# Router logits one token tile at a time, expert norms ahead of the loop, squares behind the routing steps

## The chip, the cores and the metric

The kernel runs on one core of one Trainium2 chip. The metric is the device time of one execution in microseconds (us); for the kernel before it is 814.74 us, the median of three runs (814.07 to 815.54).

## What is computed

Random-feature attention over 4 batches, 8 heads, 576 tokens, head size 64 with 128 features, then a mixture of 8 experts with one expert per token, then a gated feed-forward block. Cut to what matters here:

```python
def phi(x):
    proj = np.einsum('bhsd,md->bhsm', x, omega)
    sq = np.sum(x * x, axis=-1, keepdims=True) / 2.0
    h = proj - sq
    return np.exp(h - np.max(h, axis=-1, keepdims=True)) / np.sqrt(m)
kv = np.einsum('bhsm,bhsd->bhmd', phi(k), v);  z = np.sum(phi(k), axis=2)
x = einsum(phi(q), kv) / (einsum(phi(q), z) + 1e-06)      # 2304 tokens x 512
logits = (x / (norm(x) + 1e-6)) @ (emb / (norm(emb) + 1e-6)).T / tau   # 8 experts
expert_idx = argmax(logits);  gate_w = softmax(logits)[expert_idx]
y = gate_w * (relu(x @ w1[e]) @ w2[e])
out = (silu(y @ w_gate) * (y @ w_val)) @ w_out
```

## The kernel before, in words

The program has three phases. The first (attention and routing) fills about the first 150 us, the second (experts) and the third (gated block) are long streams of matmuls. Only the first is touched.

The 2304 tokens are 18 tiles of 128, in two groups of nine. The first phase is one hand-ordered loop of slots s = 0, 1, 2, ...; the order written in it is the order of each engine's queue. A slot takes one unit of work: nine k tiles of the first group (slots 0 to 8), nine q tiles (9 to 17), nine k tiles of the second group (18 to 26), nine q tiles (27 to 35), then a few slots that only finish older units. For unit s:

- `project` (L433): PE multiplies the tile with omega into a pair of PSUM banks ("two", two buffers).
- `squares` (L399, L403): POOL squares the tile two slots early and, from unit 6 on, adds the squares of each head pairwise from 64 down to 16 columns; `norms` (L412) reduces them on DVE into sh. Before the squares, POOL copies one column of a tile that DVE writes (`mark`, L396), and so waits until DVE has come that far: in the kernel before, until the bias of slot s.
- `maxima` (L443, L448, L451): DVE takes the maximum over the features (mx) and makes the bias; `exps` (L460): ACT makes the features ph.
- k units: `kv_sum` one slot later (L474, PE) accumulates kv; the tile in the middle of a group (MID) belongs to two batches and is done in two halves, one after the other.
- q units: `turn` (L507, PE) transposes ph into two banks of the pool "one" (two buffers); `turned` (L512) copies one bank on DVE and one on ACT (qt); `numerators` (L525, PE) two slots after the projection into the pair "third" (one buffer); `divide` (L536, L539, L540, DVE) makes the token rows x; three slots after, `turn_x` (L554, PE) transposes x, ACT rounds it (L557) and DVE takes the rest (`turned_x`, L561), which gives xp, the hi and lo halves in fp32r.

The router is woven into these slots. `router_stationary` makes the normalised expert matrix en_st: ACT squares emb (L178), then 17 small DVE instructions on 8 partitions (three Newton steps of a root, L144 to L182), one step a slot from slot 2 on; its fp32r halves stand in 16 of 128 columns, the rest are zeros (L166). The class `Routing` multiplies three tiles of xp at a time with en_st (`products`, L218, 384 columns, eight matmuls), copies 16 rows out (L225, lt), transposes them (`logits`, L230) and copies them (L233, lg), all in banks of the pool "one". From slot 21 on one step a slot of `rest` runs on DVE: the norm of the tokens (root_eps again, L144 to L159 on 9 columns), the scaled logits, the first maximum, the gates and the counts, the latter up to slot 34. The names qt, x, xp, lt, lg, mx, bias, sh, ny, nt and mark are those of the rows below.

DMAs are all issued by SP: omega, the k and v tiles, then tau and emb.

Of the kernel before, what the change touches and what calls it, by code (L numbers as in the profile page):

```python
# [10 lines left out]
F32 = mybir.dt.float32  # L11
# [16 lines left out]
def attention_moe_ffn_kernel(  # L28
# [110 lines left out]
    def root_eps(sumsq, parts, n, tag):  # L139


        y = rt.tile([128, n], F32, tag="ny" + tag, name="ny")[:parts]
        t = rt.tile([128, n], F32, tag="nt" + tag, name="nt")[:parts]
        nc.vector.tensor_scalar(  # L144
            out=y.bitcast(I32), in0=sumsq.bitcast(I32), scalar1=1, scalar2=None,
            op0=ALU.logical_shift_right,
        )
        nc.vector.tensor_scalar(
            out=y, in0=y, scalar1=0.97 * 2.0 ** 63.5, scalar2=1e-30, op0=ALU.mult, op1=ALU.max
        )  # L150
        for _ in range(3):
            yield
# [11 lines left out]
    def router_load():  # L164
        nc.sync.dma_start(out=rtau, in_=tau.partition_broadcast(128))
        nc.vector.tensor_copy(  # L166
            en_st.rearrange("p c m -> p (c m)"), zero.to_broadcast([128, NC * 128])
        )
        es = rt.tile([E, DM], F32, name="es")
        nc.sync.dma_start(out=es, in_=emb)  # L170
        return es

    def router_stationary(es):

        e2 = rt.tile([E, DM], F32, name="e2")
        ess = rt.tile([128, 1], F32, name="ess")
        nc.vector.reciprocal(rtau, rtau)
        nc.scalar.activation(out=e2, in_=es, func=AF.Square, accum_out=ess[:E])  # L178
# [4 lines left out]
        yield  # L183
        while clock[0] < PT + 4:
            yield
# [9 lines left out]
    class Routing:  # L195


        def __init__(self, g):
            self.g = g
            self.whole = False  # L200
            self.lg2 = self.small("lg2", PT, 2 * E)

# [3 lines left out]
        def scales(self):  # L206
            g = self.g
            rn = self.rn = yield from root_eps(ss[:, g * PT:(g + 1) * PT], 128, PT, "x")
            yield
            nc.vector.reciprocal(rn, rn)  # L210
            nc.vector.tensor_scalar(out=rn, in0=rn, scalar1=rtau, scalar2=None, op0=ALU.mult)

        def products(self, j):
            c0 = (self.g * PT + 3 * j) * 128
            self.p = bank_of(j == 2 and self.g == 0, 1, 384)[:, 0]
            for c in range(NC):
                for a in range(2):
                    nc.tensor.matmul(  # L218
                        self.p, en_st[:, c, :], xp[:, c, a, c0:c0 + 384],
                        start=(c == 0 and a == 0), stop=(c == NC - 1 and a == 1),  # L220
                    )

        def products_out(self):
            self.lt = rt.tile([2 * E, 384], F32, tag="lt", name="lt", bufs=2)
            nc.vector.tensor_copy(self.lt, self.p[0:2 * E])  # L225

        def logits(self, j):
            p = bank_of(j > 0 and self.g == 0, 3, 2 * E)
            for i in range(3):
                nc.tensor.transpose(  # L230
                    p[:, i, :], self.lt[:, i * 128:(i + 1) * 128], ident[:2 * E, :2 * E]
                )
            nc.vector.tensor_copy(self.lg2[:, 3 * j:3 * j + 3], p)  # L233
            self.whole = j == 2

# [3 lines left out]
        def softmax(self):  # L239
            lg2 = self.lg2  # L240
            lg = self.lg = self.small("lg", PT, E)
            nc.vector.tensor_tensor(out=lg, in0=lg2[:, :, 0:E], in1=lg2[:, :, E:2 * E], op=ALU.add)
# [3 lines left out]
            yield  # L246
            first_max(lm, self.oh, lg, PT, "t")
            yield
            nc.vector.tensor_tensor(out=lg, in0=lg, in1=self.bc(lm), op=ALU.subtract)
            nc.scalar.activation(out=lg, in_=lg, func=AF.Exp)  # L250
# [114 lines left out]
    with p1:  # L365
# [25 lines left out]
        def squares(s, after=None):  # L391
# [72 lines left out]

        def kv_part(s, bt, rows, first, last):
            ph, vt = st[s]["ph"], loads["v", units[s][1]]
            if first and bt % 2:
                a = third()
                acc[bt] = [a[:, j, 0:384] for j in range(2)]
            elif first:  # L470
                acc[bt] = [bank(384) for j in range(2)]
            for h in range(H):
                for f in COLS:
                    nc.tensor.matmul(  # L474
                        acc[bt][h // 4][f, h % 4 * 96:h % 4 * 96 + VW],
                        ph[rows, h, f], vt[rows, h * VW:(h + 1) * VW],
                        start=(first and h % 4 == 0), stop=last, skip_group_check=True,
                    )

        def kv_sum(s):  # L480
            g, i = divmod(units[s][1], PT)
            if i <= MID:
                kv_part(s, 2 * g, slice(0, 128 if i < MID else 64), i == 0, i == MID)
            if i >= MID:
                kv_part(s, 2 * g + 1, slice(0 if i > MID else 64, 128), i == MID, i == PT - 1)

# [29 lines left out]
        def numerators(s):  # L516

            a = third()
            st[s]["a"] = a[:, :, 0:384].rearrange("p a (h w) -> p a h w", w=96)
# [30 lines left out]

        def turn_x(s):
            p = st[s]["xt"] = bank_of(units[s][1] == PT - 1, NC, 128)
            for c in range(NC):
# [11 lines left out]
        om_raw = wk.tile([128, 2 * M], F32, tag="omr", name="om_raw", bufs=1)  # L565
        nc.sync.dma_start(out=om_raw, in_=om)
        load(0)
# [5 lines left out]
        load_v(2)  # L573
        emb_t = router_load()

# [11 lines left out]
        with tc.manual_schedule():  # L587
            p = third()
            for _ in range(8):
# [3 lines left out]
                out=om_s, in0=om_raw, scalar1=SCALE, scalar2=None, op0=ALU.mult  # L593
            )
            squares(0)
            squares(1)
            router = router_stationary(emb_t)
            rest = route[0].rest()
            for s in range(N + 3):
                clock[0] = s  # L600
# [12 lines left out]
                if s < LEAN:  # L613
                    sums(s)
                t = tile_of(s - 6, "q")
                if t is not None and t % 3 == 2:
                    route[-1].logits(t % PT // 3)
                base = s - (2 * PT + 2)
                if base >= 1:
                    next(rest, None)  # L620
                if base == PT + 4:
                    route.append(Routing(1))
                if old is not None:
                    turn_x(s - 3)
                t = tile_of(s - 4, "q")
                group = t is not None and t % 3 == 2
                if group:
                    route[-1].products(t % PT // 3)
                if s > 1:
                    next(router, None)  # L630
# [8 lines left out]
                if group:  # L639
                    route[-1].products_out()  # L640
                if s == PT + 4:
                    next(router, None)
                if tile_of(s - 2, "q") is not None:
# [10 lines left out]
        rest = route[1].rest()  # L654
        route[1].products(2)
        route[1].products_out()
        for _ in range(5):
            next(rest)
        route[1].logits(2)

# [319 lines left out]
```

## Time and profile before

| what | value |
|---|---|
| median of three runs | 814.74 us |
| the profiled execution | 813.87 us |
| its span | 812.1 us |
| PE busy | 792.5 us |
| DVE busy | 524.9 us |
| ACT busy | 273.6 us |
| POOL busy | 190.7 us |
| mean granted PE clock | 0.995 |

The profile's times run from the first instruction of the span; the execution itself is 1.8 us longer than the span. A line of a timeline gives start, duration, engine, source line, operation, output and inputs, shape, and in brackets how long the engine stood idle before it and what ended that. PE durations are latencies of a pipelined engine, so what a stream of matmuls costs is read from the start of one line to the start of the next.

### The profile page before, as it was taken

The page shows a single profiled execution, that of the slowest core. Times are in us where ns is not written, and L with a number is a line of the kernel's source. Part 1 is how long each engine was busy: PE and PEld are TensorE (multiplying, and loading weights), DVE is VectorE, ACT ScalarE, POOL GpSimd, SP SyncE. Part 2 cuts the span into 40 slices and gives each one's busy share as a digit, 9 for nine tenths or more (in the row PEclk, how much of TensorE's full clock was granted, in tenths as well). Part 3 has the DMA queues.
Part 4 walks back from the last instruction along what each step waited for, and adds up shares of the span by engine and source line. Part 5 has one row for each costly group of instructions (what it writes and reads, how often), then busy time and mean ns, then how long its engine had stood idle before and what let it go on. Part 6 is the DMA issues. An engine that isn't in the chain of part 4 may idle for free.

```text
span 812.1 us, 14130 instructions
## 1 busy us (share of the span) xinstructions
PE 792.5 (98%) x5788; PEld 698.8 (86%) x5789; DVE 524.9 (65%) x913; ACT 273.6 (34%) x629; POOL 190.7 (23%) x225
## 2 busy tenths in 40 slices
PE   9999989999999998999999999999999999999998
PEld 8778867899999998998888888888888888888886
DVE  5888989682433433689980079629945993797354
ACT  5798577531322315323233332112212221211120
POOL 3755573300000007222231021202111121111020
PEclk9999999999999999999999999999999999999999
DMA  7645742232423232231220011101200220020014
GB/s 272 201 140 155 224 132 81 64 111 83 101 92 94 79 68 96 89 105 54 77 78 1 0 42 63 53 0 53 78 27 0 79 78 1 26 78 27 1 52 182
DMA packets 23538, 65.69 MB, mean 81 GB/s; under 512 B 3088, under 2 KB 5664, under 8 KB 23464
## 3 DMA queue, kind: packets, MB, share of 16 engines
q1 hardware_dynamic: 23464, 64.69, 25.6%
q8 instruction: 48, 0.79, 0.4%
q14 instruction: 26, 0.21, 0.1%
HBM read 59.89 MB, written 4.79 MB: 80 GB/s over the span
## 4 chain that ended last, share of the span: by engine, by line
PE 61%; DVE 0%; issue 0%
PE two L893 24%; PE one L866 18%; PE third L893 12%; PE two L699 3%; PE third L719 2%; PE two L719 2%; PE third L699 1%; DVE y_acc L875 0%
## 5 line engine op out<-in xcount | busy, mean ns | idle before, releaser
L893 PE MATMUL two<-xp,wp 128*128 128x512 f32 (+1 forms) x960 | 209.5, 368 | 0.0
L893 PEld LDWEIGHTS two<-xp,wp 128*128 128x128 f32 x960 | 168.1, 188 | 31.4 <-DVE s L900 0.6
L866 PE MATMUL one<-wo,h 128*128 128x512 f32 x648 | 159.8, 390 | 0.0
L90 POOL TENSOR_TENSOR h<-s,h 128x512 fp32r<-128x512 f32 (+1 forms) x60 | 78.1, 1303 | 337.7 <-ACT h L89 337.7
L866 PEld LDWEIGHTS one<-wo,h 128*128 128x128 f32 x648 | 120.6, 188 | 24.8 <-DVE y_acc L875 0.3
L875 DVE TENSOR_TENSOR y_acc<-y_acc,one 128x512 f32<-128x512 f32 x90 | 61.5, 684 | 77.3 <-PE one L866 77.1
L893 PE MATMUL third<-xp,wp 128*128 128x512 f32 (+1 forms) x480 | 106.5, 368 | 0.0
L893 PEld LDWEIGHTS third<-xp,wp 128*128 128x128 f32 x480 | 84.4, 188 | 15.4
L460 ACT ACTIVATE ph<-two,bias 128x128 f32<-128x128 f32 x288 | 78.3, 385 | 34.4 <-DVE bias L451 21.2
L699 PE MATMUL two<-xp,wp 128*128 128x288 f32 x576 | 81.8, 300 | 3.7 <-DVEq L784 3.7
L699 PEld LDWEIGHTS two<-xp,wp 128*128 128x128 f32 x576 | 79.2, 192 | 3.9 <-ACT xp L89 3.9
L89 ACT CAST h<-s 128x512 fp32r<-128x512 f32 (+1 forms) x60 | 34.7, 579 | 77.6 <-DVE s L900 77.6
L90 POOL TENSOR_TENSOR xp<-y_f,xp 128x576 fp32r<-128x576 f32 x12 | 19.7, 1678 | 150.7 <-ACT xp L89 150.7
L89 ACT CAST wp<-raw 128x1024 fp32r<-128x1024 f32 x32 | 33.6, 1049 | 63.1 <-PE two L719 35.1
L900 DVE TENSOR_TENSOR s<-two,s 128x512 f32<-128x512 f32 (+1 forms) x40 | 25.3, 633 | 44.3 <-ACT s L899 44.2
L719 PE MATMUL third<-h,wp 128*128 128x288 f32 x384 | 52.5, 296 | 0.0
L899 ACT ACTIVATE s<-two 128x512 f32<-128x512 f32 (+1 forms) x40 | 22.2, 554 | 89.0 <-PE two L893 89.0
L719 PE MATMUL two<-h,wp 128*128 128x288 f32 x384 | 51.8, 296 | 0.0
L719 PEld LDWEIGHTS third<-h,wp 128*128 128x128 f32 x384 | 51.6, 189 | 0.0
L719 PEld LDWEIGHTS two<-h,wp 128*128 128x128 f32 x384 | 51.4, 189 | 0.0
L90 DVE TENSOR_TENSOR wp<-raw,wp 128x1024 fp32r<-128x1024 f32 x30 | 39.1, 1302 | 15.6 <-ACT wp L89 15.6
L443 DVE TENSOR_REDUCE mx<-two 128x8 f32<-128x1024 f32 x36 | 43.8, 1216 | 8.1 <-PE two L433 7.9
(155 smaller groups left out, 927.2 us busy)
## 6 DMA issues: line engine op xcount, KB each, us to landing
raw<-in_w_dram SPq DMA_DIRECT2D x68, 512.0 KB, 3.5
q<-in_qx_dram SPq DMA_DIRECT2D x18, 512.0 KB, 3.6
k<-in_kx_dram SPq DMA_DIRECT2D x14, 512.0 KB, 4.6
v<-in_vx_dram SPq DMA_DIRECT2D x18, 276.0 KB, 4.2
out_dram<-y_acc SPq DMA_DIRECT2D x18, 256.0 KB, 2.0
gate<-gts SPq DMA_DIRECT2D x4, 256.0 KB, 5.3
k<-in_kx_dram SPq DMA_DIRECT2D x3, 256.0 KB, 4.1
k<-in_kx_dram SPq DMA_DIRECT2D x2, 128.0 KB, 2.4
```

Of the source, the lines that this page charges most:

```text
L89: nc.scalar.copy(hi, src)
L90: lo_eng.tensor_tensor(out=lo, in0=src, in1=hi.bitcast(F32), op=ALU.subtract)
L443: nc.vector.tensor_reduce(out=mx.rearrange("p (c a) -> p a c", a=2), in_=p.rearrange("p a (h m) -> p a h m", m=M), axis=AX.X, op=ALU.max,)
L460: nc.scalar.activation(out=ph[:, h, :], in_=p[:, h % 2, h // 2 * M:(h // 2 + 1) * M], func=AF.Exp, bias=bias[:, h:h + 1],)
L699: nc.tensor.matmul(ps[:, j], w[:, a, c, f * 128:(f + 1) * 128], xp[:, c, b, c0 + j * HB:c0 + (j + 1) * HB], start=(c == 0 and n == 0), sto ...
L719: nc.tensor.matmul(ps[:, j], w[:, a, f, :], h[:, b, j * HB:(j + 1) * HB], start=(f == 0 and n == 0), stop=(f == len(hs) - 1 and n == 2),)
L866: nc.tensor.matmul(p, h[:, x, i * 128:(i + 1) * 128], w[:, a, :], start=(k == 0), stop=(k == 3 * GF - 1),)
L875: nc.vector.tensor_tensor(out=dst, in0=dst, in1=p, op=ALU.add)
L893: nc.tensor.matmul(ps[:, m], w[:, a, m, c, :], xp[:, c, x, cols], start=(k == 0), stop=(k == 3 * NC - 1),)
L899: nc.scalar.activation(out=s, in_=ps[:, 0], func=AF.Silu)
L900: nc.vector.tensor_tensor(out=s, in0=ps[:, 1], in1=s, op=ALU.mult)
```

## The change

Six edits of the first phase:

1. omega, tau and emb are issued by ACT's queue, ahead of ACT's table load; SP's queue starts with the first k tile. The zero fill of en_st goes, en_st has 16 columns.
2. The root of the expert norms runs before the slots: ACT squares emb, then squares units 0 and 1 (POOL did these two), and DVE's 17 small instructions stand before the first maximum. The transposes of the expert matrix come at slot 11 and not 13.
3. The router takes one tile a slot: eight fp32r matmuls with 16 stationary columns and 128 moving ones (`products`), one copy of 16x128, one transpose, and one reduction of both halves to eight logits, in columns of the pair "third" that the numerators leave free (384 to 511, and 360 to 375 of its second bank). "third" is taken before the tile's transposes and given to the numerators later in the slot. The last tile of a group is transposed into "third" too.
4. `rest` makes two steps a slot up to slot 26, and POOL's `mark` waits for what that step wrote, if there was one, and not for the bias.
5. Units 23 to 28 keep the full 64 squares a head: POOL adds nothing up, DVE reduces 512 columns.
6. In the MID tile the matmuls of the two batches alternate between column halves of the array.

```diff
-    en_st = rt.tile([128, NC, 128], F32R, name="en_st")
+    en_st = rt.tile([128, NC, 2 * E], F32R, name="en_st")
...
-        nc.sync.dma_start(out=rtau, in_=tau.partition_broadcast(128))
-        nc.vector.tensor_copy(
-            en_st.rearrange("p c m -> p (c m)"), zero.to_broadcast([128, NC * 128])
-        )
+        nc.scalar.dma_start(out=rtau, in_=tau.partition_broadcast(128))
         es = rt.tile([E, DM], F32, name="es")
-        nc.sync.dma_start(out=es, in_=emb)
+        nc.scalar.dma_start(out=es, in_=emb)
...
-        while clock[0] < PT + 4:
+        nc.vector.reciprocal(rtau, rtau)
+        while clock[0] < PT + 2:
...
-        def products(self, j):
-            c0 = (self.g * PT + 3 * j) * 128
-            self.p = bank_of(j == 2 and self.g == 0, 1, 384)[:, 0]
+        def products(self, t, a):
+            self.p = a[0:2 * E, 1, 384:]
             for c in range(NC):
-                for a in range(2):
+                for b in range(2):
                     nc.tensor.matmul(
-                        self.p, en_st[:, c, :], xp[:, c, a, c0:c0 + 384],
+                        self.p, en_st[:, c, :], xp[:, c, b, t * 128:(t + 1) * 128],
...
+        def logits(self, a):
+            self.q = a[:, 1, 360:360 + 2 * E]
+            nc.tensor.matmul(
+                self.q, self.lt, ident[:2 * E, :2 * E], is_transpose=True,
+                start=True, stop=True, skip_group_check=True,
+            )
+        def logits_out(self, t):
+            i = t - self.g * PT
+            nc.vector.tensor_reduce(
+                out=self.lg[:, i], in_=self.q.rearrange("p (a e) -> p e a", a=2),
+                axis=AX.X, op=ALU.add,
+            )
...
-            nc.gpsimd.tensor_tensor(out=sq, in0=xn, in1=xn, op=ALU.mult)
+            if s < 2:
+                nc.scalar.activation(out=sq, in_=xn, func=AF.Square)
+            else:
+                nc.gpsimd.tensor_tensor(out=sq, in0=xn, in1=xn, op=ALU.mult)
             w = D
-            while w > (D // 4 if s > 5 else D):
+            while w > (D // 4 if s > 5 and not 2 * PT + 5 <= s < 3 * PT + 2 else D):
...
-                for f in COLS:
+                for f in range(2):
+                    for n, (bt, rows, first, last) in enumerate(parts):
+                        cols = COLS[(f + n) % 2]
...
-            for s in range(N + 3):
+            for _ in range(4):
+                next(router)
+            for s in range(N + 5):
...
+                wrote = None
                 if base >= 1:
-                    next(rest, None)
+                    for _ in range(2 if s < 3 * PT else 1):
+                        wrote = next(rest, None)
...
+                t, u = tile_of(s - 4, "q"), tile_of(s - 5, "q")
+                inner = tile_of(s - 2, "q") is not None
+                if inner or old is not None or t is not None or u is not None:
+                    a = third()
                 if old is not None:
-                    turn_x(s - 3)
+                    turn_x(s - 3, a)
+                if u is not None:
+                    route[u // PT].logits(a)
+                if t is not None:
+                    route[t // PT].products(t, a)
...
-                    squares(s + 2, st[s]["bias"])
+                    squares(s + 2, st[s]["bias"] if wrote is None else wrote)
...
+                if inner:
+                    st[s - 2]["third"] = a
+                    numerators(s - 2)
+                if t is not None:
+                    route[t // PT].products_out()
+                if u is not None:
+                    route[u // PT].logits_out(u)
+                if inner:
                     divide(s - 2)
```

On DVE at the start of the program, the rows before (ess is the sum of the squared expert rows, om_s the scaled omega):

```order
L166 CAST en_st<-zero 128x512
L592 TENSOR_SCALAR om_s<-om_raw 128x256
L443 TENSOR_REDUCE mx<-two 128x2x4
L448 SCALAR_TENSOR_TENSOR mx<-third,mx 128x2x4
L451 SCALAR_TENSOR_TENSOR bias<-third,mx 128x2x4
```

and the rows now, from the third Newton step on (the rows ahead of these are om_s, the first two steps and the root's start, L144 and L148):

```order
L153 RECIPROCAL nt<-ny 8x1
L154 TENSOR_TENSOR nt<-nt,ess 8x1
L155 TENSOR_TENSOR ny<-ny,nt 8x1
L156 TENSOR_SCALAR ny<-ny 8x1
L159 TENSOR_SCALAR ny<-ny 8x1
L177 RECIPROCAL ny<-ny 8x1
L178 TENSOR_SCALAR es<-es,ny 8x512
L449 TENSOR_REDUCE mx<-two 128x2x4
L454 SCALAR_TENSOR_TENSOR mx<-third,mx 128x2x4
L457 SCALAR_TENSOR_TENSOR bias<-third,mx 128x2x4
```

All seventeen instructions of the expert norms have moved ahead of the first maximum; before, they stood between slots 3 and 7.

On DVE in a q slot, with the waits, the rows before in a slot that ends a group of three tiles:

```order
L451 SCALAR_TENSOR_TENSOR bias<-sh,mx 128x2x4 [waits DVE_49]
L561 TENSOR_TENSOR xp<-one,xp 128x4x128 [waits Activation_49]
L225 COPY lt<-one 16x384 [waits PE_49]
L536 TENSOR_SCALAR r<-third 128x8 [waits PE_49]
L539 RECIPROCAL r<-r 128x8 [waits DVE_49]
L540 TENSOR_TENSOR x<-third,r 128x512 [waits DVE_49]
```

and now in every q slot from slot 14 on:

```order
L457 SCALAR_TENSOR_TENSOR bias<-sh,mx 128x2x4 [waits DVE_49]
L578 TENSOR_TENSOR xp<-one,xp 128x4x128 [waits Activation_49]
L223 COPY lt<-third 16x128 [waits PE_49]
L235 TENSOR_REDUCE lg<-third 128x8
L548 TENSOR_SCALAR r<-third 128x8
L551 RECIPROCAL r<-r 128x8 [waits DVE_49]
L552 TENSOR_TENSOR x<-third,r 128x512 [waits DVE_49]
```

The wait for the numerators has moved from r to lt: r, which reads the numerators, waits for nothing of its own any more, so the copy lt stands until PE has written them.

On POOL in slots 21 and 22, the rows before:

```order
L396 COPY mark<-bias 128x1
L399 TENSOR_TENSOR sq<-k_1389 128x512
L403 TENSOR_TENSOR sq<-sq 128x8x32
L403 TENSOR_TENSOR sq<-sq 128x8x16
L396 COPY mark<-bias 128x1
L399 TENSOR_TENSOR sq<-k_1476 128x512
L403 TENSOR_TENSOR sq<-sq 128x8x32
L403 TENSOR_TENSOR sq<-sq 128x8x16
```

and now, in slots 21 to 24:

```order
L399 COPY mark<-ny 128x1
L405 TENSOR_TENSOR sq<-k_1431 128x512
L399 COPY mark<-ny 128x1
L405 TENSOR_TENSOR sq<-k_1530 128x512
L399 COPY mark<-oh 128x1
L405 TENSOR_TENSOR sq<-k_1602 128x512
L399 COPY mark<-bias 128x1
L405 TENSOR_TENSOR sq<-k_1672 128x512
```

The squares now wait for ny or oh, which DVE's routing step of that slot writes before the maximum, and the two additions are gone there.

## Rows read from the trace of the kernel before

**Rows 1.** Windows of the first phase and after: us, busy time by engine, granted clock, DMA.

```profile
37.46:81.41 43.95, 41.19 (x611) 34.49 (x611) 38.23 (x90) 37.65 (x122) 24.85 (x43) 1.00 0.48 150
81.41:112.90 31.49, 29.63 (x471) 24.85 (x471) 28.85 (x71) 20.00 (x74) 20.27 (x35) 0.95 0.64 195
112.90:141.48 28.58, 25.42 (x361) 20.90 (x358) 25.78 (x73) 23.47 (x76) 12.93 (x22) 1.00 0.29 95
150.00:200.00 50.00, 50.00 (x400) 49.53 (x399) 28.86 (x72) 17.55 (x26) 4.65 (x3) 1.00 0.34 102
```

**Rows 2.** Start: timelines of DVE, ACT and SP; then DMA issues (KB each, us to landing).

```profile
6.02 1.23 DVE L443 TENSOR_REDUCE mx<-two 128x8 f32<-128x1024 f32 x1 [2.80 <-PE two L433]
...
11.85 0.61 ACT L178 ACTIVATE e<-es 8x512 f32<-8x512 f32 x1
...
1.22 1.37 SPq L380 DMA_DIRECT2D k<-in_kx_dram  x3
...
om_raw<-in_om_dram SPq DMA_DIRECT2D x1, 128.0 KB, 2.1
...
rtau<-in_tau_dram SPq DMA_DIRECT2D x1, 0.5 KB, 5.8
```

**Rows 3.** Timeline of DVE, maxima of slots 9 and 11.

```profile
34.41 1.23 DVE L443 TENSOR_REDUCE mx<-two 128x8 f32<-128x1024 f32 x1 [0.55 <-PE two L433]
...
40.06 1.23 DVE L443 TENSOR_REDUCE mx<-two 128x8 f32<-128x1024 f32 x1
```

**Rows 4.** Timeline of DVE, a q slot without router work.

```profile
68.97 0.68 DVE L561 TENSOR_TENSOR xp<-one,xp 128x512 fp32r<-128x512 f32 x1
69.58 0.15 DVE L536 TENSOR_SCALAR r<-third 128x8 f32<-128x8 f32 x1
...
70.61 0.68 DVE L512 COPY qt<-one 128x512 f32<-128x512 f32 x1
71.21 0.28 DVE L412 TENSOR_REDUCE sh<-sq 128x8 f32<-128x128 f32 x1
...
73.06 0.68 DVE L561 TENSOR_TENSOR xp<-one,xp 128x512 fp32r<-128x512 f32 x1
```

**Rows 5.** Router on DVE, 37.46 to 81.41: a copy; waits (total, times, longest).

```profile
59.71 0.54 DVE L225 COPY lt<-one 16x384 f32<-16x384 f32 x1
...
DVE r L536 <- PE third L525: 1.5, 3, 0.7
...
DVE lg L233 <- PE third L230: 1.1, 1, 1.1
```

**Rows 6.** Timeline of PE, a q slot that ends a group of three tiles.

```profile
57.44 0.66 PE L554 MATMUL one<-ident,x 128*128 128x128 f32 x4
57.85 1.67 PE L218 MATMUL one<-xp,en_st 128*128 128x384 f32 x8
59.45 1.15 PE L525 MATMUL third<-kv,qt 128*64 128x65 f32 x32
60.53 1.09 PE L507 MATMUL one<-ident,ph 128*128 128x128 f32 x8
61.55 1.16 PE L433 MATMUL two<-om_s,q 64*128 64x128 f32 x16
```

**Rows 7.** Timeline of PE, fp32r matmuls of 256 columns in the third phase.

```profile
780.51 3.04 PE L893 MATMUL third<-xp,wp 128*128 128x256 f32 x24
```

**Rows 8.** DVE busy by tile and window: ny, cand; nt in two windows.

```profile
81.41:112.90 31.49, 5.99 (x15) 0.95 0.64 195
...
81.41:112.90 31.49, 1.93 (x4) 0.95 0.64 195
...
81.41:112.90 31.49, 3.11 (x9) 0.95 0.64 195
...
157.00:180.00 23.00, 1.61 (x9) 1.00 0.44 129
```

**Rows 9.** Timeline of POOL, squares of a tile in the second k stretch.

```profile
102.22 1.10 POOL L399 TENSOR_TENSOR sq<-q 128x512 f32<-128x512 f32 x1
```

More of the change, by code (lines that the diff above doesn't have):

```diff
@@ L200, in __init__ @@
             self.whole = False
-            self.lg2 = self.small("lg2", PT, 2 * E)
+            self.lg = self.small("lg", PT, E)
         def small(self, name, *shape):
@@ L208, in scales @@
             rn = self.rn = yield from root_eps(ss[:, g * PT:(g + 1) * PT], 128, PT, "x")
-            yield
+            yield rn
             nc.vector.reciprocal(rn, rn)
             nc.vector.tensor_scalar(out=rn, in0=rn, scalar1=rtau, scalar2=None, op0=ALU.mult)
-        def products(self, j):
-            c0 = (self.g * PT + 3 * j) * 128
-            self.p = bank_of(j == 2 and self.g == 0, 1, 384)[:, 0]
+        def products(self, t, a):
+            self.p = a[0:2 * E, 1, 384:]
             for c in range(NC):
-                for a in range(2):
+                for b in range(2):
                     nc.tensor.matmul(
-                        self.p, en_st[:, c, :], xp[:, c, a, c0:c0 + 384],
-                        start=(c == 0 and a == 0), stop=(c == NC - 1 and a == 1),
+                        self.p, en_st[:, c, :], xp[:, c, b, t * 128:(t + 1) * 128],
+                        start=(c == 0 and b == 0), stop=(c == NC - 1 and b == 1),
+                        skip_group_check=True,
                     )
         def products_out(self):
[L224 to L234, printed above, removed]
+            self.lt = rt.tile([2 * E, 128], F32, tag="lt", name="lt", bufs=2)
+            nc.vector.tensor_copy(self.lt, self.p)
+        def logits(self, a):
[10 more added lines that the diff above has]
+            )
+            self.whole = i == PT - 1
         def bc(self, t):
@@ L463, in exps, with kv_parts @@
                 )
-        def kv_part(s, bt, rows, first, last):
+        def kv_parts(s, parts):
             ph, vt = st[s]["ph"], loads["v", units[s][1]]
[L467 to L471, printed above, removed]
-            for h in range(H):
-                for f in COLS:
[L474 to L478, printed above, removed]
+            for bt, _, first, _ in parts:
+                if first and bt % 2:
+                    a = third()
+                    acc[bt] = [a[:, j, 0:384] for j in range(2)]
+                elif first:
+                    acc[bt] = [bank(384) for j in range(2)]
+            for h in range(H):
+                for f in range(2):
+                    for n, (bt, rows, first, last) in enumerate(parts):
+                        cols = COLS[(f + n) % 2]
+                        nc.tensor.matmul(
+                            acc[bt][h // 4][cols, h % 4 * 96:h % 4 * 96 + VW],
+                            ph[rows, h, cols], vt[rows, h * VW:(h + 1) * VW],
+                            start=(first and h % 4 == 0), stop=last, skip_group_check=True,
+                        )
         def kv_sum(s):
             g, i = divmod(units[s][1], PT)
+            parts = []
             if i <= MID:
-                kv_part(s, 2 * g, slice(0, 128 if i < MID else 64), i == 0, i == MID)
+                parts.append((2 * g, slice(0, 128 if i < MID else 64), i == 0, i == MID))
             if i >= MID:
-                kv_part(s, 2 * g + 1, slice(0 if i > MID else 64, 128), i == MID, i == PT - 1)
+                parts.append((2 * g + 1, slice(0 if i > MID else 64, 128), i == MID, i == PT - 1))
+            kv_parts(s, parts)
         def kv_out(s):
@@ L516, in numerators @@
         def numerators(s):
-            a = third()
+            a = st[s]["third"]
             st[s]["a"] = a[:, :, 0:384].rearrange("p a (h w) -> p a h w", w=96)
@@ L549, in token_norms, with turn_x @@
             nc.scalar.activation(out=x2, in_=st[s]["x"], func=AF.Square, accum_out=ss[:, t:t + 1])
-        def turn_x(s):
-            p = st[s]["xt"] = bank_of(units[s][1] == PT - 1, NC, 128)
+        def turn_x(s, a):
+            if units[s][1] == PT - 1:
+                p = a[:, 0].rearrange("p (c t) -> p c t", c=NC)
+            else:
+                p = bank(NC, 128)
+            st[s]["xt"] = p
             for c in range(NC):
@@ L594, in attention_moe_ffn_kernel @@
             )
+            router = router_stationary(emb_t)
+            next(router)
             squares(0)
             squares(1)
-            router = router_stationary(emb_t)
+            for _ in range(4):
+                next(router)
             rest = route[0].rest()
-            for s in range(N + 3):
+            for s in range(N + 5):
                 clock[0] = s
```

37 lines of the change are left out of this document (9 added, 28 removed).

## The prediction

> **What bounds the kernel now.** I read the windows by stage first. From 150 us on PE is busy all the time [rows 1], so nothing that happens in the first phase can be hidden or regained later: the change is worth what it moves the end of that phase, us for us. The borders of the other windows are the starts of the maxima of slots 10, 20, 29 and 35, so a window is a number of slot intervals: ten, nine and six. In all three DVE is the busiest engine by share of work that it cannot overlap with itself (38.2 of 43.95, 28.9 of 31.5, 25.8 of 28.6); PE's 41.2 of 43.95 is a sum of pipelined latencies and reads too high.
>
> Then the timelines. A q slot without router work runs from one xp to the next on DVE in 73.06 - 68.97 = 4.09 us without a gap [rows 4]: DVE sets the pace there. PE needs, in a q slot that holds a group's products, 61.55 - 57.44 = 4.11 from turn_x to the next projection, and some 1.1 for the projection itself (its row has 1.16); the products are 59.45 - 57.85 = 1.60 of it [rows 6]. So PE without router work needs 3.6 a slot and has half a us to spare. A k slot is bound by a ring of PE, DVE and ACT: from the maximum of slot 9 to that of slot 11 it took 40.06 - 34.41 = 5.65, 2.8 a slot, and DVE waited for PE [rows 3]. Wherever k slots take longer than 2.8, DVE has other work in them: the router's small instructions. Those are far dearer than their size. The nine that touch nt took 3.11 us in the second k stretch, beside POOL's squares, and 1.61 for the second group, where POOL does none [rows 8], so 0.18 each when free.
>
> **The sum, stage by stage.** All prices are from the one profiled execution, 813.87 us, which is 0.87 under the median of 814.74; differences are put on the median.
>
> *Start.* The first maximum stands at 6.02 [rows 2]. Now DVE does the 17 instructions of the expert norms ahead of it: 16 at 0.18 [rows 8] and one over 512 columns, priced like lt's 0.54 for 384 [rows 5], make 3.4. They wait for ACT's square of emb, 0.61 [rows 2] and the read of its sum, together some 0.8, and that for emb's landing. emb is third on ACT's queue; three issues on SP took 1.37 [rows 2], so it is issued near 1.7. Landing takes between omega's 2.1 and tau's 5.8 [rows 2]; tau goes just ahead of emb on the same queue, but the queues are nearly empty then, so I take 2.8, near omega's. Maximum at 1.7 + 2.8 + 0.8 + 3.4 = 8.7 (8.0 to 11.7): **+2.7** (+2.0 to +5.7). Squares 0 and 1 on ACT and the missing zero fill lie beside that wait and cost nothing; if emb came at once, project(0) would be the cover.
>
> *First k slots.* From the maximum of slot 0 to that of slot 10 are 37.46 - 6.02 = 31.44. Without the norms between them the slots fall to the ring: five pairs at 5.65, 28.2 in all: **-3.2**. Start and these together are -0.5, between -1.2 and +2.5. The alternating MID matmuls are in the 5.65.
>
> *First q slots (ten intervals, 43.95).* Away go, for the two groups in this window, two copies lt, of 0.54 each with 0.07 overlapped, two copies lg at 0.13, 1.2 in all, and of the waits that DVE has [rows 5] the 1.1 for lg and 0.8 of the 1.5 for r (the other 0.7 is the first numerators' and stays): 3.1. New are, in some 6.5 slots, a copy of 16x128 and a reduction to 8 columns. The trace has neither; between sh's 0.28 for 128 columns [rows 4] and the smallest instructions' 0.18 [rows 8] they are 0.21 and 0.13, 0.34 a slot, 2.2. That makes DVE 4.09 + 0.34 = 4.43 a slot.
>
> Whether PE keeps up with that rests on one price: eight fp32r matmuls of 128 columns. The nearest rows: 24 of 256 columns take 3.04, 0.12 each [rows 7], and a column at the granted clock of 1.00 (2.4 GHz) is 0.42 ns, so 107 of those 120 ns are columns. Taking 256 columns off each of the eight of 384 leaves 1.60 - 0.85 = **0.75**, switches from and to fp32 included. From above: an fp32 transpose of 128 columns takes 1.02 / 8 = 0.128 [rows 6], and a full fp32 product is two passes (the projection's eight matmuls leave 16 records), so eight at full fp32 price would be 2.05. I take 0.75: nothing in 256 or 384 columns departs from one column a cycle. PE then needs 3.6 + 0.75 + 0.1 for one transpose = 4.45. The wait that the change adds: lt stands on DVE until the numerators are written, and r, x, and the next qt are queued behind lt. That makes a ring: qt 0.60 (70.61 to 71.21), turn_x 0.41, transpose 0.1, products 0.75, numerators 1.08 (59.45 to 60.53), lt and lg 0.34, r to x 1.03 (69.58 to 70.61) [rows 4, 6], with 0.2 for three handovers: 4.5. So the slots run at 4.5, 0.08 over DVE's own, 0.5 in six. Window: -3.1 + 2.2 + 0.5 = **-0.4**.
>
> On that added wait: "PSUM — Partial Sum Buffer" of the Trainium skill (section Terms) says that TensorE writing and VectorE reading one bank in one quadrant at the same time is an error. No run here shows it; the order of the instructions agrees, since lt waits for the numerators of its own bank. By a rule that let lt go first, the sum would be 0.7 lower.
>
> *Second k slots (nine intervals, 31.49).* The router's steps there suffered from the squares: the 15 instructions with ny took 5.99 where 15 at 0.2 are 3.0, those with nt 1.5 too much, the four with cand 1.0 [rows 8]: 5.5. With `mark` behind the step, POOL's squares of 1.10 us [rows 9] start under the maximum of 1.23 [rows 3], and I let all 5.5 go. In come sixteen small instructions that stood in slots 29 to 34, at 0.2: +3.2; and in six slots sh from 512 columns, about 0.68 by a line through the maximum's 1.23 for 1024 columns and sh's 0.28 for 128 [rows 3, 4]: +2.4. Per-tile and group work of the router are even here. **+0.1**, between -2 and +3.
>
> *Second q slots (six intervals, 28.58).* The sixteen instructions go, -3.2, and one group's lt, lg and wait for lg, -1.1; per-tile work comes in 4.5 slots, +1.5, the ring in three, +0.3: **-2.5**.
>
> *Behind.* The tail's products and transposes fall under the experts' matmuls as before: 0. SP's queue loses three issues, which are not what its loads wait for: 0.
>
> Sum -0.5 - 0.4 + 0.1 - 2.5 = -3.3: 810.6 against 813.87 in the profile, **811** against the median. Its own range, with the bounds of start and k slots that are not rivals, is 807 to 814.
>
> **Rivals.**
> *Narrow fp32r matmuls are slow (slower).* If 128 columns cost what fp32 costs, products take 2.05 and not 0.75. PE then needs 5.75 a slot and becomes the bound, and DVE's lt stands behind it; of 18 tiles two fall into k slots with room, so 16 x 1.3 = 21 us: 832. For it: no row shows fp32r under 256 columns or with 16 stationary ones. Against: 256, 384 lie on one line. It decides from where products exceed about 0.8 a slot; at half of the way, 1.4, the time would be 821.
> *emb comes late (no change).* With tau's 5.8 us to land the first maximum is at 11.7, and 3 of the 3.3 are lost: 814. For it: tau's tiny pieces stand right ahead of emb on the queue. Against: tau's 5.8 were measured behind eight larger loads. "Trainium Kernel Development and Optimization" of the Trainium skill (section Key Constraints) says that DMAs of all queues run on the same 16 engines and interleave, so that a second issuing engine saves issue time alone; the rows of the start, where SP's issues are 0.45 apart, cannot contradict it, and by it emb shares with the first k tiles, which is this rival.
> *The squares still collide (slower).* If DVE's two-input instructions behind the maximum meet the squares instead, the 5.5 stay: 817. Against: 1.10 us of squares fit under 1.23.
>
> **Numbers.** A measurement of this kernel tells 0.2% (1.6 us) from no change. Forecast 811: 0.54. emb late, 814: 0.12. Narrow matmuls, 821 to 832: 0.27. Collision, 817: 0.07. So faster 0.54, same 0.12, slower 0.34. Cases of both signs hold most of the chance, so the range has to run from the forecast's low end, 807 (the lower bounds of start and k slots together), to the narrow matmuls' 832.
>
> **What would show it.** Right: the eight products of a tile take 0.75 on PE, q slots run at 4.5, DVE waits before lt by a tenth or two, the first maximum is at 8.7, and no routing instruction in the second k slots is over 0.3. Wrong: products near 2 us with DVE waiting over a us before lt; a first maximum past 11; bias or mx instructions of 0.6 and more beside the squares.

## The result and the profile after

| | before | after |
|---|---|---|
| median of four runs | 814.48 us (814.07 to 815.54) | 824.88 us (822.43 to 826.22) |
| ratio to before, 95% interval | | 1.0118 [1.0102, 1.0135] |
| span of the profiled execution | 812.1 us | 821.8 us |
| mean granted PE clock | 0.995 | 0.986 |
| PE busy | 792.5 us | 798.9 us |
| DVE busy | 524.9 us | 524.9 us |

The change made the kernel 1.2% slower; 811 was forecast. The span grew by 9.7 us, where -3.3 was forecast. Cut at the maxima of slots 0, 10, 20, 29 and 35, as the forecast was:

| stage | before | after | difference | forecast |
|---|---|---|---|---|
| start to first maximum | 6.02 | 8.85 | +2.8 | +2.7 |
| first k slots (0 to 10) | 31.44 | 32.51 | +1.1 | -3.2 |
| first q slots (10 to 20) | 43.95 | 46.13 | +2.2 | -0.4 |
| second k slots (20 to 29) | 31.49 | 33.09 | +1.6 | +0.1 |
| second q slots (29 to 35) | 28.58 | 28.50 | -0.1 | -2.5 |
| behind the last maximum | 670.6 | 672.7 | +2.1 | 0 |

These are the windows of the changed kernel (length; busy time and instructions of PE, PE's weight loads, DVE, ACT, POOL; granted clock; DMA share; GB/s); the last three answer to [rows 1]:

```profile
8.85:41.36 32.51, 30.68 (x513) 27.61 (x514) 19.29 (x41) 20.63 (x77) 17.40 (x30) 0.84 0.66 209
...
41.36:87.49 46.13, 43.91 (x651) 36.76 (x652) 39.14 (x99) 37.89 (x123) 25.14 (x43) 0.96 0.44 142
87.49:120.58 33.09, 27.99 (x466) 22.59 (x466) 30.35 (x87) 19.62 (x74) 12.48 (x22) 1.00 0.62 188
120.58:149.08 28.50, 27.05 (x392) 22.94 (x393) 24.25 (x62) 24.16 (x78) 13.53 (x23) 0.94 0.29 94
```

The column to read first is the third from the right, the granted clock. Before, of [rows 1] only the second k window was under 1.00 (0.95). Now the other three stages are. In 2 us windows the first of these stretches looks so:

```profile
8.00:10.00 2.00, 0.15 (x4) 0.00 (x0) 1.90 (x5) 0.00 (x0) 0.00 (x0) 1.00 1.01 380
10.00:12.00 2.00, 1.32 (x16) 1.35 (x16) 1.52 (x4) 1.37 (x6) 1.18 (x2) 0.76 0.92 332
12.00:14.00 2.00, 2.00 (x35) 1.97 (x34) 0.33 (x2) 2.00 (x9) 1.18 (x2) 0.50 0.11 39
...
20.00:22.00 2.00, 2.00 (x30) 2.00 (x28) 0.43 (x1) 0.47 (x2) 0.00 (x0) 0.68 0.52 140
```

PE does next to nothing from 8 to 10 us, then the clock is at half (1.2 GHz) for some 10 us. The timeline of DVE and PE there:

```profile
7.01 1.14 PE L439 MATMUL two<-om_s,k 64*128 64x128 f32 x16
...
8.45 0.47 DVE L178 TENSOR_SCALAR es<-es,ny 8x512 f32<-8x512 f32 x1
8.85 1.21 DVE L449 TENSOR_REDUCE mx<-two 128x8 f32<-128x1024 f32 x1
...
10.68 1.56 PE L428 MATMUL third<-ones,sq 64*128 64x1 f32 x16 [2.53 <-DVE bias L457]
...
14.11 2.08 PE L439 MATMUL two<-om_s,k 64*128 64x128 f32 x16
...
16.24 1.22 DVE L449 TENSOR_REDUCE mx<-two 128x8 f32<-128x1024 f32 x1 [3.58 <-PE two L439]
```

The norms end at 8.9, near the forecast, but PE, with the projection of slot 1 done, waits 2.53 us for the first bias. The next projection then takes 2.08 instead of 1.14, and DVE waits 3.58 for it.

A second stretch begins in slot 11, behind another wait of PE:

```profile
44.12 0.41 PE L185 MATMUL one<-ident,es 8*128 8x8 f32 x4
...
46.74 0.65 PE L519 MATMUL one<-ident,ph 128*128 128x128 f32 x4
...
48.50 0.18 DVE L188 TENSOR_TENSOR en_st<-one,en_st 128x32 fp32r<-128x32 f32 x1
...
48.64 1.12 PE L519 MATMUL one<-ident,ph 128*128 128x128 f32 x4 [1.24 <-DVE qt L524]
49.68 2.08 PE L439 MATMUL two<-om_s,q 64*128 64x128 f32 x16
```

The expert matrix is turned into one of the two banks of the pool "one" in slot 11 (L185) and frees it only with its lo half on DVE in slot 12 (L188). The second half of the turn of ph needs that bank and waits for it: the bracket names the copy qt, which DVE began at 47.90, but L188, right behind it, is what reads the bank. Slot 11, from its maximum to the next, took 7.58 us; before, 4.75.

What the forecast staked most on went well. A slot of the per-tile router:

```profile
65.36 0.65 PE L215 MATMUL third<-xp,en_st 128*16 128x128 f32 x8
...
67.15 0.28 DVE L223 COPY lt<-third 16x128 f32<-16x128 f32 x1 [0.23 <-PE third L537]
67.35 0.15 DVE L235 TENSOR_REDUCE lg<-third 128x8 f32<-128x16 f32 x1
...
69.26 1.22 DVE L449 TENSOR_REDUCE mx<-two 128x8 f32<-128x1024 f32 x1
```

Eight products take 0.65 us (0.59 to the start of the numerators), lt waits 0.23, and the next maximum follows 4.57 us after that of 64.69. In the second k slots five of DVE's small instructions are still long (oc, gt, cand and ext_i are tiles of the routing steps):

```profile
90.51 0.70 DVE L144 TENSOR_SCALAR ny<-ss 128x9 int32<-128x9 int32 x1
...
105.16 1.04 POOL L405 TENSOR_TENSOR sq<-k 128x512 f32<-128x512 f32 x1
...
105.37 0.85 DVE L266 TENSOR_TENSOR oc<-oc,oh 64x8 f32<-64x8 f32 x1
...
109.17 0.77 DVE L275 TENSOR_TENSOR gt<-oh,se 128x72 f32<-128x72 f32 x1
...
112.54 1.04 DVE L127 SCALAR_TENSOR_TENSOR cand<-cand,iota_b 128x16 f32<-128x16 f32 x1
...
116.71 0.89 DVE L309 CAST ext_i<-cnt 1x16 int32<-1x16 f32 x1
```

And behind the loop PE waits once more, in the experts' first matmuls:

```profile
170.54 3.54 PE L720 MATMUL two<-xp,wp 128*128 128x288 f32 x25
174.01 0.23 PE L228 MATMUL third<-ident,lt 16*128 16x16 f32 x1
...
174.54 3.42 PE L720 MATMUL third<-xp,wp 128*128 128x288 f32 x24
...
179.59 0.63 PE L720 MATMUL third<-xp,wp 128*128 128x288 f32 x3 [1.37 <-DVE cand L127]
```

The pair "third" belongs to the router until its last logits at 174; the experts' first "third" pair starts at 174.5 (before: 158.7), and the next one waits 1.37 us for DVE. From the last maximum to the first matmul of the second expert product (189.25) it is 40.17 us; before, 38.17.

### The profile page after: what moved, and what is told of

Read it like the earlier page. It is cut to its first block, busy times and chain, and to the rows that moved or that the text cites. A ratio compares the mean times of both kernels' runs of the same rounds, so it can differ in the third digit from the quotient of the medians.

```text
span 821.8 us, 14331 instructions
## 1 busy us (share of the span) xinstructions
PE 798.9 (97%) x5884; PEld 704.3 (86%) x5885; DVE 524.9 (64%) x934; ACT 275.0 (33%) x631; POOL 180.2 (22%) x211
## 4 chain that ended last, share of the span: by engine, by line
PE 60%; DVE 0%; issue 0%
PE two L914 24%; PE one L887 18%; PE third L914 12%; PE two L720 3%; PE third L740 2%; PE two L740 2%; PE third L720 1%; DVE y_acc L896 0%
```

## The experiments

All start from the changed kernel, but for one. Kernels sent together share the runs of the kernel before, whose median was 815.0 to 815.3 there. The number in brackets is the median of a kernel's executions; every profile is of one execution.

**PE kept busy at the start** (820.05).

```diff
                     project(s)
+                if s == 1:
+                    spare = bank(128)
+                    for _ in range(6):
+                        nc.tensor.matmul(spare, ones, ones, start=True, stop=True)
```

> The changed kernel with six full fp32 matmuls of 128x128 into a free bank behind the projection of slot 1, where PE stood idle for 2.5 us until the first bias; their product is used by nobody. Theory clock (PE's idleness behind the early norms sent the granted clock to half for 10.2 us, which is what slots 1 and 2 cost): no half-clock stretch from 11 us on, slots 1 and 2 fall from 5.79 and 5.33 us to about 3.7 and 3.0, time 824.9 - 4.4 = 820.5. Theory waits (the late first maximum itself, and the ring behind it, cost the time; the clock is a by-product): slots 1 and 2 stay above 5, time 825.

Windows of this run, over the start and from the maximum of slot 0 to that of slot 10:

```profile
8.00:10.00 2.00, 2.00 (x24) 1.88 (x22) 1.85 (x5) 0.00 (x0) 0.00 (x0) 1.00 0.96 314
10.00:12.00 2.00, 2.00 (x42) 1.81 (x41) 1.52 (x4) 1.85 (x8) 1.46 (x4) 1.00 0.81 281
12.00:14.00 2.00, 2.00 (x36) 1.81 (x36) 0.15 (x1) 2.00 (x10) 0.90 (x1) 1.00 0.72 233
...
8.37:36.61 28.24, 28.24 (x531) 24.81 (x528) 19.28 (x41) 20.60 (x77) 17.41 (x30) 1.00 0.80 251
```

Work that nobody uses made the kernel some 4.8 us faster than the change by the medians, 3 by the ratios to the kernel before (1.0080 for 1.0118), 5.0 by the spans of the profiles. Slots 1 and 2 took 3.88 and 2.96, and the ten intervals 28.24 us, the 28.2 of the forecast; in the changed kernel they took 32.51. So the wait cost little by itself, and what it did to the clock cost 4.3.

**The expert matrix in slot 7** (820.31).

```diff
-        while clock[0] < PT + 2:
+        while clock[0] < PT - 2:
...
-                if s >= PT:
+                if s >= PT - 2:
                     next(router, None)
```

> The changed kernel with the transposes of the expert matrix in slot 7 and not 11, and their lo half in slot 8. Theory bank (en_st holds one of the two banks 'one' from slot 11 until DVE comes to the lo half in slot 12, and PE's turn of slot 11 waits 1.2 us for it, after which the clock drops): slot 11 falls from 7.58 to about 4.75, no half-clock stretch at 48.6, time 824.9 - 2.8 = 822. Rival (slot 11 is long because the first numerators wait for ACT's qt behind the exponentials, whatever en_st does): slot 11 stays near 7, half clock stays, 825.

Slot 11 took 4.73, with no half clock there; the ten intervals of the first q slots 43.34, against 46.13 and, before, 43.95: -0.6 where -0.4 was forecast. The bank was the cause. The median fell by 4.6, more than the 2.8 of this slot; the profiled span fell by 3.2.

**The norms back in the slots** (818.33).

```diff
-            for _ in range(4):
-                next(router)
...
-                if s >= PT:
+                if s > 1:
                     next(router, None)
```

> The changed kernel with the expert norms' 17 DVE instructions back in slots 2 to 7, one step a slot; all else as changed. Theory clock: first maximum near 6.0, no half clock before 40 us, maximum of slot 10 at 37.5 as before and not 41.4: 824.9 - 3.9 = 821. If the early norms as I forecast them save what they cost (ring of 2.8 a slot), slots 3 to 8 lengthen by 3 us again and the time is 825 or more.

The stretch from 11 us on is gone; a shorter one came at 26 to 29 us, which the expectation had excluded. The maximum of slot 10 stood at 37.76. Faster than expected, since slot 11 had its wait but no half clock:

```profile
45.05 0.66 PE L519 MATMUL one<-ident,ph 128*128 128x128 f32 x4 [1.25 <-DVE qt L524]
45.63 1.16 PE L439 MATMUL two<-om_s,q 64*128 64x128 f32 x16
```

It took 6.19: of slot 11's 2.8 us in the changed kernel half is the wait (6.19 - 4.73 = 1.5), half the clock (7.58 - 6.19 = 1.4).

**PE kept busy in slot 29** (822.23).

```diff
             for h in range(H):
+                if s == 3 * PT and h == 4:
+                    for _ in range(3):
+                        nc.tensor.matmul(
+                            a[:, 0, 384:], ones, ones, start=True, stop=True, skip_group_check=True
+                        )
```

> The changed kernel with three full fp32 matmuls of 128x128 into spare columns between the two halves of the first numerators of the second group (slot 29), where PE waits 1.37 us for ACT's qt. Theory clock: no half-clock stretch at 123.7, slot 29 falls from 6.40 to about 4.6, time 824.9 - 1.9 = 823. Theory waits: slot 29 stays near 6.4 or grows by the matmuls' 1.2, time 825 to 826.

Slot 29 took 4.94 at full clock, against 6.40 at half. But it took 4.93 and 4.94 in three other kernels without the fill too, whose half-clock stretches lay elsewhere. So the stretch costs 1.5 in this slot; that the fill took it away is not shown.

**Marks behind the routing steps** (821.59). In slots 24 to 27 POOL's mark waits for what the step wrote last:

```diff
-                yield
+                yield oc[:, j - 1] if j else oh[:, 0]
...
-            yield
+            yield cnt[:, 0]
...
-            yield
+            yield dom[:, 0]
```

> The changed kernel, POOL's order alone different: in slots 24 to 27 mark waits for what the routing step of the slot wrote last (oh, oc, cnt, dom) and not for the bias. Theory locks (the four instructions L266 0.85, L275 0.77, L127 1.04 and L309 0.89 us are slow because the squares of the slot before still run beside them; 0.2 each when free): three of the four fall to 0.2 to 0.25 and slots 24 to 27 shorten by 0.6 to 0.8 each, about 2 in all: 824.9 - 2.0 = 823, the maximum of slot 29 2 us earlier against that of slot 20. Rival (they are slow for a reason of their own, such as a 64-partition or a narrow operand): durations and time unchanged. A second rival: squares that come earlier collide with other small instructions instead: less than 1 us.

On DVE's timeline the last four instructions of above are now (the first, L144, stays at 0.70), and ahead of them one has become long:

```profile
102.89 0.69 DVE L454 SCALAR_TENSOR_TENSOR mx<-sh,mx 128x8 f32<-128x8 f32 x1
...
106.68 0.16 DVE L266 TENSOR_TENSOR oc<-oc,oh 64x8 f32<-64x8 f32 x1
...
111.04 0.23 DVE L275 TENSOR_TENSOR gt<-oh,se 128x72 f32<-128x72 f32 x1
...
114.34 0.17 DVE L127 SCALAR_TENSOR_TENSOR cand<-cand,iota_b 128x16 f32<-128x16 f32 x1
...
118.05 0.16 DVE L309 CAST ext_i<-cnt 1x16 int32<-1x16 f32 x1
```

All four fell, so their length was the squares beside them. "SBUF — State Buffer" of the Trainium skill (section Who interferes with whom) says that VectorE, with two inputs in SBUF or in the modes that use two ports, and GpSimd share one pair of ports, which one of them holds for a whole instruction; these rows agree. But the squares that start earlier meet the instruction behind the maximum of slot 23: L454 took 0.17 in the changed kernel, and the slot grew from 2.68 to 3.20. The nine intervals gained only 0.3, 32.79 for 33.09, and this execution had a half-clock stretch at 106 to 110; with the same order and none (all remedies, below) they took 31.75. So the marks are worth 1.3 at full clock, not 2.

**The router's tail in "one"** (818.24).

```diff
-                    a = third()
+                    a = third() if s < N + 2 else bank(1, 512)
```

> The changed kernel with the last three routing slots of the second group (behind the last numerators) in a bank of the pool 'one' and not in 'third'. Theory shared pair (the experts' first 'third' pair cannot start until the router's last logits are out, 174.5 us here and 158.7 before, so two 'third' pairs stand back to back and PE waits 1.4 us for the first to be emptied): first mm2 38.2 to 38.7 us behind the last maximum and not 40.2, time 824.9 - 1.7 = 823. Rival (the tail's extra 2 us are PE's own work for 16-column products and transposes): still 40, time 825.

The experts' first two "third" pairs on PE are apart again, and nothing waits:

```profile
162.94 2.96 PE L720 MATMUL third<-xp,wp 128*128 128x288 f32 x21
...
173.67 3.36 PE L720 MATMUL third<-xp,wp 128*128 128x288 f32 x24
```

The tail fell from 40.17 to 38.50, so 1.7 of its 2.0 was the shared pair. The time fell by more. In the profiled execution the half-clock stretch at the start was shorter than in that of the changed kernel (slots 1 and 2: 5.04 and 2.96) and slot 29 had none (4.93), and no edit explains that.

**POOL's additions back in units 23 to 28** (820.07).

```diff
-            while w > (D // 4 if s > 5 and not 2 * PT + 5 <= s < 3 * PT + 2 else D):
+            while w > (D // 4 if s > 5 else D):
```

> The changed kernel with POOL's two additions back in units 23 to 28, so that DVE reduces 128 columns and not 512 there. By the forecast's prices DVE saves 0.40 in each of six slots (sh 0.27 for 0.67) and POOL's additions, 1.25 us a slot more, meet the small instructions of the next slot. Theory locks: the collisions cost as much as sh saves or more, time 825 to 827. Rival (full-width sh was the dearer choice): 823.

The second k slots took 34.26 for 33.09, a half-clock stretch at 99 to 106 among them. Two slots ahead of it were 0.5 and 0.4 longer for another reason: the squares with their additions outlast the maximum and meet the instruction behind it, 0.17 us elsewhere:

```profile
89.24 1.21 DVE L449 TENSOR_REDUCE mx<-two 128x8 f32<-128x1024 f32 x1
90.48 0.72 DVE L454 SCALAR_TENSOR_TENSOR mx<-sh,mx 128x8 f32<-128x8 f32 x1
```

The four slots behind the stretch were 0.8 shorter together, with DVE reducing 128 columns for 512. So outside the stretch the two orders come out nearly even, and which width is cheaper is not shown: the two slots in the stretch, 1.0 longer, make the difference. The whole time, 820, came out below both theories for other reasons: the half-clock stretch at the start was shorter than in the changed kernel, and slots 11 and 29 had none (6.21 and 4.94).

**The late maximum alone, on the kernel before** (818.01, ratio 1.0052 [1.0034, 1.007]).

```diff
+            scr = wk.tile([128, 1], F32, name="scr", bufs=1)
+            nc.vector.memset(scr, 1.0)
+            for _ in range(31):
+                nc.vector.tensor_scalar(
+                    out=scr, in0=scr, scalar1=1.0, scalar2=None, op0=ALU.mult
+                )
             router = router_stationary(emb_t)
```

> The kernel BEFORE the change with nothing of the change, only 31 small DVE instructions on a scratch tile ahead of the first maximum, so that it stands near 8.8 us and not at 6.0, as in the changed kernel. Theory clock: PE then stands idle for some 2.5 us behind the projection of slot 1, the granted clock falls to half for about 10 us from 10 or 11 us on, and slots 1 and 2 take some 10 us together where they took 6.7: 814.7 + 2.8 + 3 = 820 to 821. Theory waits (a late first maximum costs its own 2.8 us, and DVE's cover behind it gives part of that back): no half clock, 816 to 817.5.

```profile
8.00:10.00 2.00, 0.00 (x0) 0.00 (x0) 1.83 (x7) 0.00 (x0) 0.00 (x0) 1.00 0.58 192
10.00:12.00 2.00, 1.16 (x20) 1.18 (x22) 1.74 (x5) 1.21 (x5) 1.18 (x2) 0.95 0.99 397
12.00:14.00 2.00, 2.00 (x34) 1.88 (x36) 0.34 (x3) 2.00 (x9) 1.18 (x2) 0.50 0.58 234
14.00:16.00 2.00, 2.00 (x28) 2.00 (x30) 0.35 (x1) 1.50 (x6) 0.00 (x0) 0.70 0.51 128
```

With nothing of the change in it, the clock goes to half behind a PE that is idle for 3.0 us, for some 3.4 us in this execution and not 10. Slot 1 took 5.04 for 3.72, the maximum of slot 10 came 4.1 later, 3.0 of it by the later first maximum. The time lies between the two theories; the executions ran from 817.92 to 821.08.

**The router by token tile without the other reorderings** (816.87, 1.0019 [1.0008, 1.0030]). Norms back, expert matrix in slot 8, one routing step a slot, mark behind the bias, additions in all units.

> The changed kernel with the other edits of DVE's and POOL's order undone: norms in slots 2 to 7, squares of units 0 and 1 on POOL, one routing step a slot, mark behind the bias, additions in all units; expert matrix in slot 8. What is left is the router by token tile, the alternating MID matmuls and the issues on ACT. By the forecast's terms (0.75 us of products, slots of 4.5): the loop ends 0.5 to 1.5 us earlier than before, and the tail, which still holds 'third' to the end, gives 2 back: 815 to 816. If the per-tile router itself were the loss: 820 or more.

The last maximum stood at 141.53, before at 141.48: the first q slots -0.6, the second k slots +0.5, the second q slots +0.1. The per-tile router is worth nothing in the loop as a whole in this execution, which had a half-clock stretch at 26 to 29 us, in the first k slots; its tail, 40.19, costs the 2 us. A little slower than expected.

**All remedies** (813.11, 0.9985 [0.9968, 1.0002]): start and slot 29 filled, expert matrix in slot 7, marks, tail.

> The changed kernel with all remedies at once: fill at the start, expert matrix in slot 7, fill in slot 29, marks behind the routing steps, tail in 'one'. If the causes add: 824.9 - 4.4 - 2.8 - 1.9 - 2.0 - 1.7 = 812, under the kernel before (814.5). The half-clock stretches move with every shift of the start, so where one of them falls on PE's path elsewhere, 1.5 to 2 more: 814. If the remedies cover the same time twice: 817.

Its windows behind slot 10, with the granted clock at 1.00; the profile shows no other value in the first phase:

```profile
36.99:80.31 43.32, 41.87 (x647) 35.20 (x648) 38.99 (x98) 37.60 (x122) 25.05 (x43) 1.00 0.48 151
80.31:112.06 31.75, 28.16 (x470) 22.82 (x472) 28.60 (x88) 19.76 (x75) 12.55 (x22) 1.00 0.65 196
112.06:138.90 26.84, 26.24 (x398) 22.24 (x399) 24.33 (x60) 23.81 (x77) 13.33 (x23) 1.00 0.32 100
```

The profiled execution took 811.69 us, 2.2 under that of the kernel before, where -3.3 was forecast; others took up to 817.67. By stages it differs from the kernel before by -0.5 (start and first k slots), -0.6, +0.3, -1.7 and +0.4; the forecast had -0.5, -0.4, +0.1, -2.5 and 0. So at full clock, and with these remedies, the forecast's sum comes out within about 1 us in that execution. As a median the kernel cannot be told from the kernel before.

**The same, and slot 11 filled** (814.06, 0.9999 [0.9980, 1.0018]).

> All remedies as in the run with all at once, and three matmuls more between the halves of the first numerators of the first group (slot 11, where PE still stood idle for 1.3 us). Theory clock: the executions with a half-clock stretch near 45 us become fewer; median 812.5, 0.3% under the kernel before. Rival (slot 11 has nothing to do with those executions): 813.1 as without them.

No gain: twelve executions ran from 810.20 to 818.64, with granted clocks of 0.998 to 0.989.

**All remedies, slot 11 filled, but without the early norms** and without the fill at the start, expert matrix in slot 8 (813.61, 0.9987 [0.9976, 0.9997]).

> All remedies but the early norms: the 17 instructions in slots 2 to 7, no fill at the start. By the forecast the early norms save 0.5 us once PE is kept busy; the run with norms back alone has its maximum of slot 10 at 37.8 and the one with the fill at 36.6, so 1.1: 813 + 1.1 = 814. If the fill's matmuls only move the half-clock stretch elsewhere, no difference: 813.

Ten executions ran from 812.21 to 814.82. The maximum of slot 10 stood at 36.85, between those of the two runs before this one (36.99 and 36.56); as a median it is no slower. So with PE kept busy the early norms gain nothing that shows over norms in the slots. This is the one kernel here whose interval lies under the kernel before, by 0.13%, less than the 0.2% that the forecast took for the least difference to tell.

## Why the prediction was wrong

**Start (+2.7): right, and its end too.** The first maximum stood at 8.85 for 8.7.

**First k slots, "the slots fall to the ring: five pairs at 5.65, 28.2 in all: -3.2": the step that failed.** It is right at full clock (28.24 with PE kept busy) and took PE's pace from rows at a clock of 1.00. That DVE's 3.4 us would leave PE idle for 2.5, and what an idle PE does to the clock, had no term and no rival, though [rows 1] had a window at 0.95. It cost 4.3 of the 13 us between forecast and result, the largest single part. "TensorE: Matmul & The Clock Gate" of the Trainium skill (section What's actually happening) says that half speed is the clock's default state and activity releases it; the run on the kernel before agrees in that the clock fell behind an idle PE and rose with PE busy, and the page would have given a rival here. Nor is the net of -0.5 for start and k slots the norms' doing: with them in the slots the maximum of slot 10 came at 36.85, as early as with them moved and PE kept busy, and before at 37.46. That 0.6 must be due to other edits; the alternating MID matmuls and the issues on ACT's queue were never run alone.

**First q slots (-0.4): products right, one edit not costed.** Products 0.65 for 0.75, slots 4.57 for 4.5, lt's wait 0.23, window -0.6 once the expert matrix is moved. That the transposes of the expert matrix move to slot 11 stands in the change and in no term: 2.8 us, half of it a wait for a bank held over two slots, half the clock.

**Second k slots (+0.1): "I let all 5.5 go" held for what it named, not for what comes in.** The instructions on ny and nt fell from 9.10 us [rows 8] to 5.00 (six stand in both sums), 4.1 of their 4.5; one, at 0.70, stayed long. But of the steps moved in, priced at 0.2 an instruction, several give no tile to `mark`; the squares then start behind the bias and run into the next slot's step. Four instructions took 3.55 us so, and 0.72 when free, on a term that forecast no such cost. Of these 2.8 the window gets back 1.3 (33.09 to 31.75), since another instruction then meets the squares; 31.75 is +0.3, near the forecast.

**Second q slots (-2.5):** -0.1 with the half-clock stretch, which costs 1.5 (27.04 without it, with PE kept busy at the start); with all remedies -1.7 (26.84). The missing 0.8 is not traced.

**Behind (0): wrong by 2.** I followed the router's work on PE and not who takes the pair next: 1.7 of it is "third" given to the experts 16 us later (the run with the tail in "one").

**Rivals.** Narrow fp32r matmuls are not slow: a tile's 0.59 to 0.65 lies under the 0.75 of the forecast. emb did not come late: ACT's square of it began at 4.80. The squares' rival named the wrong victims in the changed kernel: not the two-input instructions behind the maximum, but the next slot's step; with the marks behind every step it named the right one (L454, 0.69). That the result lies in the range is luck: it is owed to the narrow matmuls' upper end, a mechanism that did not occur. (The lower end, by its own bounds of -0.7 and -2.1, would be 808 and not 807.)

Left open: why a half-clock stretch is short in one execution and three times as long in another; why waits of 1.0 to 1.4 us, as in slot 11, are followed by one in some executions and not in others; and where the longer executions of the two kernels with early norms and all remedies lose their time; there is one profile of each.

## What to carry to other kernels

When an edit makes TensorE wait at a place where its pace counts, price the wait twice: once as a wait, once as what follows at half clock; and where work has to stand ahead of the first matmuls' consumers, let TensorE do something meanwhile or leave that work in the loop. Here the first was worth some 4 us at the start, and in slots 11 and 29 no gain from it is shown. Follow each buffer that an edit touches to its next owner, across the end of the phase. An order that shields small VectorE instructions from GpSimd has to cover every step, or the rest pay; and what is shielded in one place can be met in another.

## What the runs showed of the hardware

In seven profiles PE stood idle at the start for 1.6 to 3.0 us, and in each half clock followed, for about 3.4 to 10 us, with PE busy; the longest wait had one of the shortest stretches. In the others, where PE waited there for 0.5 us at most, none followed. At half, a projection took 2.08 us for 1.14. What a stretch costs depends on the slots: in the second k slots nothing while DVE's long instructions stood in them (33.12 with a stretch and PE kept busy at the start, 33.09 without), and 0.8 to 1.1 with the marks (32.51 to 32.83 in three kernels, for 31.75). The profile's granted clock can miss a stretch at the very start: with all remedies it shows 1.00 from 4 to 8 us, and the first projection took the time that others took at half:

```profile
4.81 2.08 PE L439 MATMUL two<-om_s,k 64*128 64x128 f32 x16
```

Eight fp32r matmuls of 128 columns and 16 stationary ones took 0.59 us from their start to the start of what follows, 74 ns each. A cast of 16 elements on one partition took 0.89 us beside POOL's squares and 0.16 without them.
